# Cached attention on one core: the permutation of P moves from the normalization to the exponential's write and to the transposes' read

## The chip, the cores and the metric

The kernel runs on one core of a Trainium2 chip. The metric is the device time of one execution in microseconds (us); every time below is of that kind or comes from one profiled execution. Five engines work side by side, each through its own queue in order: TensorE (PE, with its weight loads shown apart as PEld), VectorE (DVE), ScalarE (ACT), GpSimd (POOL) and the queue SP, which here only issues transfers. They are held together by semaphores.

## The reference

There are two blocks, A and B, of the same form, and their outputs are put side by side. For each block, with 16 batches, 64 query rows, model width 640, 32 heads of 128 and 512 cached keys:

```python
q = (x @ wq).reshape(B, Sq, H, Dh).transpose(0, 2, 1, 3)
scores = einsum("bhqd,bhkd->bhqk", q, k_cache) * (Dh ** -0.5)
p = softmax(scores, axis=-1)
o = einsum("bhqk,bhkd->bhqd", p, v_cache)
out = o.transpose(0, 2, 1, 3).reshape(B, Sq, H * Dh) @ wo
```

All inputs and the output are bf16.

## The kernel before

Two batches are taken together, so that 2 x 64 query rows fill 128 partitions. One step g is one head of such a pair; two steps make a macro step m. There are 256 macro steps: 2 blocks x 2 halves of 16 heads x 8 pairs of batches x 8 macro steps. Every 8 macro steps a new group (a new pair of batches, or a new half or block) begins.

The order of each engine's work is written out by hand. A template per engine (class Cfg, lines 30 to 33) lists what the engine does in one slot and, beside each entry, how many macro steps ahead of the slot it works:

```python
PE_T = (("TR2", 1), ("QP2", 4), ("KX", 4, 0), ("SM2", 3), ("PV2", 1), ("XT", 0), ("OP2", 0), ("KX", 4, 1))
ACT_T = (("QE2", 4), ("OE2", 1), ("XE", 0), ("EX", 3, 0), ("EX", 3, 1), ("OV", 0), ("ST", -1))
DVE_T = (("TE2", 1), ("RC2", 2), ("KE", 4, 0), ("MX", 3, 0), ("MX", 3, 1), ("KE", 4, 1), ("OVF", 0))
POOL_T = (("NM", 0, 0), ("NM", 0, 1))
```

In the order of the data, for one macro step:

- KX (line 433) transposes the cached keys on TensorE, 8 tiles for each of the two batches; KE (line 442) copies them out of PSUM on VectorE.
- QP2 (line 451) projects the queries, QE2 (line 459) copies them out on ScalarE with the scale.
- SM2 (line 467) makes the scores of the two steps into two PSUM banks, one for each step (s_bank, line 424). There are only these two banks, so SM2 of the next macro step can begin only when both exponentials of this one have read them.
- MX (line 476, VectorE) takes the negated row maximum, one instruction for each step.
- EX (line 482, ScalarE) takes the exponential with that maximum as bias, writes P to p_ring in bf16 and sums the rows into rowsum; on the chip it is two instructions, an ACTIVATE and a short read of the accumulator.
- RC2 (line 488, VectorE) takes the reciprocals of both sums.
- NM (line 496, GpSimd) multiplies P with the reciprocal into pn_ring, one instruction for each step.
- TR2 (line 505) transposes 128 columns of pn_ring at a time, 4 tiles for each step, into PSUM; the tile of pn_ring is the stationary operand of these matrix products, which a weight load brings in, and the identity is streamed. TE2 (line 512, VectorE) copies the result out.
- PV2 (line 524) multiplies with the cached values, OE2 (line 532, ScalarE) copies out, OP2 (lines 540 and 545) projects into the output banks.
- XT (line 604) and XE (line 612) transpose the rows of x and copy them out on ScalarE, once for each group, so in 32 of the 256 slots.

The order of keys matters here. The keys come in so that column t x 64 + pp of the scores is key 8 pp + t (t below 8, pp below 64). The values come in so that partition p of tile t' holds key 4 p + t'. So the columns of P have to be put in another order on their way from the scores to the transposes. In this kernel NM does that: it reads P as it lies, (th, tl, pp), and writes pn_ring in the order (tl, pp, th), which is a step of 4 bytes between elements that are written one after the other. EX writes without a step, and TR2 loads 128 columns that lie side by side.

Of the kernel before, what the change touches and what calls it, by code (L numbers as in the profile page):

```python
# [7 lines left out]
ACTF = mybir.ActivationFunctionType  # L8
ALU = mybir.AluOpType
# [5 lines left out]
class Cfg:  # L15
# [9 lines left out]
    NP = 4  # L25
    NPN = 3
# [320 lines left out]
def mha_kernel(nc, blocks, out, cfg=None):  # L347
# [8 lines left out]
    scale = float(DH) ** -0.5  # L356
# [9 lines left out]
    NKB, NVB, NX, NXN, NQ, NKT, NP, NPN, NT, NO, NR = (cfg.NKB, cfg.NVB, cfg.NX, cfg.NXN, cfg.NQ, cfg.NKT, cfg.NP,  # L366
                                                       cfg.NPN, cfg.NT, cfg.NO, cfg.NR)
# [10 lines left out]
    with contextlib.ExitStack() as es:  # L378
        block = es.enter_context(nc.Block())

        def sb(name, shape, dt):
            return es.enter_context(nc.sbuf_tensor(name, shape, dt))
# [10 lines left out]
        p_ring = sb("p_ring", [128, NP, SK], BF16)  # L393
        pn_ring = sb("pn_ring", [128, NPN, SK], BF16)
# [3 lines left out]
        negmax = sb("negmax", [128, NR], F32)  # L398
        rowsum = sb("rowsum", [128, NR], F32)
        recip = sb("recip", [128, NR], F32)  # L400
        ones_sb = sb("ones_sb", [128, 128], BF16)
        ident = sb("ident", [128, 128], BF16)
# [15 lines left out]
        pt_ps = pt_ps_flat.rearrange("p (s t q) -> p s t q", s=2, t=4)  # L418
# [5 lines left out]
        def s_bank(sub):  # L424
            return ps[:, S_BANK0 + sub, :]
# [53 lines left out]
        def em_EX(e, op):  # L479
            g = op.idx  # L480
            r = g % NR
            ins = e.activation(p_ring[:, g % NP, :], s_bank(g % 2), ACTF.Exp, bias=negmax[:, r:r + 1], scale=1.0,  # L482
                               accum_out=rowsum[:, r:r + 1])
            return ins, ins

# [5 lines left out]
        def em_NM(e, op):  # L491
            g = op.idx
            r = g % NR
            src = p_ring[:, g % NP, :].rearrange("q (th tl pp) -> q th tl pp", th=2, tl=4)
            dst = pn_ring[:, g % NPN, :].rearrange("q (tl pp th) -> q th tl pp", tl=4, th=2)
            ins = e.tensor_scalar(dst, src, recip[:, r:r + 1], 1.0, ALU.mult, ALU.mult)  # L496
            return ins, ins

        def em_TR2(e, op):
            m = op.idx  # L500
            first = last = None
            for sub in range(2):
                g = 2 * m + sub
                for t in range(4):
                    ins = e.transpose(pt_ps[:, sub, t, :], pn_ring[:, g % NPN, t * 128:(t + 1) * 128], ident[:, :])  # L505
                    first = first or ins
                    last = ins
            return first, last
# [107 lines left out]
        def em_LDKV(e, op):  # L616
# [6 lines left out]
            else:  # L623
# [3 lines left out]
            return ins, ins  # L627

        emitters = dict(KX=em_KX, KE=em_KE, QP2=em_QP2, QE2=em_QE2, SM2=em_SM2, MX=em_MX, EX=em_EX, RC2=em_RC2,
                        NM=em_NM, TR2=em_TR2, TE2=em_TE2, PV2=em_PV2, OE2=em_OE2, OP2=em_OP2, OV=em_OV,  # L630
                        OVP=em_OVP, OVF=em_OVF, ST=em_ST, XT=em_XT, XE=em_XE, INIT1=em_INIT1, INIT2=em_INIT2,
                        LDWQ=em_LDWQ, LDWO=em_LDWO, LDX=em_LDX, LDK=em_LDKV, LDV=em_LDKV)
# [87 lines left out]
```

## Time and profile before

| | |
|---|---|
| time, median of 2 runs | 958.55 us (958.49 and 958.61) |
| span of the profiled execution | 956.8 us |
| mean granted TensorE clock | 0.998 of full speed |
| ScalarE busy | 567.1 us (59%) |
| GpSimd busy | 416.9 us (44%) |
| VectorE busy | 841.9 us (88%) |
| HBM | 311 GB/s over the span |
| copy of the values' transposes, line 512, mean | 682 ns |
| copy of queries, 128x256, line 459, mean | 384 ns |
| copy of x, 128x640 to bf16, line 612, mean | 702 ns |
| copy of partial outputs, 128x640 to f32, line 555, mean | 710 ns |
| read of the accumulator after EX, mean | 205 ns |
| weight load of any 128x128 tile, mean | 98 to 99 ns |

The span is the time from the first to the last instruction in one profiled execution; the timed runs are other executions, 1.7 to 1.8 us above it. A weight load overlaps the matrix products and the next loads, so its mean duration is not what one costs: the distance from one load to the next is. [...]

### The profile page before, as it was taken

The page shows a single profiled execution, that of the slowest core. Times are in us where ns is not written, and L with a number is a line of the kernel's source. Part 1 is how long each engine was busy: PE and PEld are TensorE (multiplying, and loading weights), DVE is VectorE, ACT ScalarE, POOL GpSimd, SP SyncE. Part 2 cuts the span into 40 slices and gives each one's busy share as a digit, 9 for nine tenths or more (in the row PEclk, how much of TensorE's full clock was granted, in tenths as well). Part 3 has the DMA queues.
Part 4 walks back from the last instruction along what each step waited for, and adds up shares of the span by engine and source line. Part 5 has one row for each costly group of instructions (what it writes and reads, how often), then busy time and mean ns, then how long its engine had stood idle before and what let it go on. Part 6 is the DMA issues. An engine that isn't in the chain of part 4 may idle for free.

```text
span 956.8 us, 34351 instructions
## 1 busy us (share of the span) xinstructions
PE 919.4 (96%) x14755; PEld 733.5 (77%) x15008; DVE 841.9 (88%) x1552; ACT 567.1 (59%) x1585; POOL 416.9 (44%) x518
## 2 busy tenths in 40 slices
PE   4999999999999999999999999999999999999997
PEld 3877777778777777877777787777877778777775
DVE  2898899898899999899999899889899998999996
ACT  1666656666665565656566666666666656565654
POOL 0444444444444444444444444444444444444443
PEclk9999999999999999999999999999999999999999
DMA  9999999999999999888999999988888988899830
GB/s 315 364 365 364 351 365 367 365 368 351 338 337 337 343 330 315 299 292 305 322 332 352 326 353 327 306 294 296 302 305 288 308 301 297 295 297 314 295 124 15
DMA packets 230871, 299.51 MB, mean 313 GB/s; under 512 B 9536, under 2 KB 165184, under 8 KB 230720
## 3 DMA queue, kind: packets, MB, share of 16 engines
q1 hardware_dynamic: 228416, 294.69, 91.0%
q8 instruction: 118, 1.93, 0.8%
q10 hardware_dynamic: 2304, 2.62, 0.8%
q14 instruction: 33, 0.27, 0.1%
HBM read 294.65 MB, written 2.62 MB: 311 GB/s over the span
## 4 chain that ended last, share of the span: by engine, by line
PE 89%; DVE 4%; POOL 3%; issue 2%; SPq 1%; DMA 1%; POOLq 0%; DVEq 0%
PE ps L433 22%; PE ps L524 14%; PE ps L451 14%; PE ps L467 14%; PE ps L505 12%; PE ps L545 7%; PE ps L540 5%; POOL pn_ring L496 3%; DVE out_sb L560 1%; DVE ktp_ring L442 1%; DVE pT_ring L512 1%; PE ps L604 1%; DMA xn_ring<-in_A_x_dram 1%; SPq L626 1%; SPq L583 1%
## 5 line engine op out<-in xcount | busy, mean ns | idle before, releaser
L496 POOL TENSOR_SCALAR pn_ring<-p_ring,recip 128x512 bf16<-128x512 bf16 x512 | 416.3, 843 | 532.7 <-DVE recip L488 532.7
L442 DVE COPY ktp_ring<-ps 128x1024 bf16<-128x1024 bf16 x512 | 353.7, 691 | 105.3 <-PE ps L433 85.1
L482 ACT ACTIVATE p_ring<-ps,negmax 128x512 bf16<-128x512 f32 x512 | 345.6, 684 | 4.8 <-DVE negmax L476 4.8
L476 DVE TENSOR_REDUCE negmax<-ps 128x1 f32<-128x512 f32 x512 | 327.3, 681 | 0.4 <-PE ps L467 0.3
L433 PE MATMUL ps<-ident,kn_ring 128*128 128x128 bf16 x4096 | 314.6, 220 | 2.8 <-DMA kn_ring<-in_A_k_cache_dram 1.6
L532 ACT ACTIVATE oT_ring<-ps 128x256 bf16<-128x256 f32 x256 | 98.0, 383 | 306.0 <-PE ps L524 306.0
L433 PEld LDWEIGHTS ps<-ident,kn_ring 128*128 128x128 bf16 x4096 | 251.9, 98 | 34.2 <-DVE ktp_ring L442 2.6
L524 PEld LDWEIGHTS ps<-pT_ring,v_ring 128*128 128x128 bf16 x4096 | 133.5, 98 | 109.2 <-issue 100.0
L451 PE MATMUL ps<-xT_ring,wq_sb 128*128 128x128 bf16 x2560 | 186.4, 220 | 3.2 <-DMA wq_sb<-in_A_wq_dram 3.2
L512 DVE COPY pT_ring<-ps 128x1024 bf16<-128x1024 bf16 x256 | 174.5, 682 | 4.6 <-PE ps L505 3.8
L524 PE MATMUL ps<-pT_ring,v_ring 128*128 128x64 bf16 x4096 | 163.8, 194 | 3.3 <-issue 1.7
L467 PE MATMUL ps<-ktp_ring,qT_ring 128*64 128x512 bf16 x1024 | 159.8, 392 | 0.4 <-ACT p_ring L482 0.4
L505 PE MATMUL ps<-ident,pn_ring 128*128 128x128 bf16 x2048 | 156.7, 219 | 3.5 <-POOL pn_ring L496 3.5
L451 PEld LDWEIGHTS ps<-xT_ring,wq_sb 128*128 128x128 bf16 x2560 | 155.2, 98 | 3.5 <-DMA wq_sb<-in_A_wq_dram 3.5
L459 ACT ACTIVATE qT_ring<-ps 128x256 bf16<-128x256 f32 x256 | 98.4, 384 | 66.8 <-PE ps L451 66.8
L505 PEld LDWEIGHTS ps<-ident,pn_ring 128*128 128x128 bf16 x2048 | 124.1, 98 | 7.0 <-POOL pn_ring L496 6.7
L545 PE MATMUL ps<-wo_sb,oT_ring 128*128 128x128 bf16 x512 | 112.1, 219 | 13.4
L482 ACT ACTIVATION_READ_ACCUMULATOR p_ring<-ps,negmax 128x1 f32 x512 | 105.0, 205 | 0.0
L540 PE MATMUL ps<-wo_sb,oT_ring 128*128 128x512 bf16 x259 | 97.8, 379 | 0.0
L540 PEld LDWEIGHTS ps<-wo_sb,oT_ring 128*128 128x128 bf16 x512 | 50.1, 98 | 30.6 <-ACT oT_ring L532 0.3
L467 PEld LDWEIGHTS ps<-ktp_ring,qT_ring 128*64 128x64 bf16 x1024 | 36.1, 108 | 27.1 <-ACT p_ring L482 0.6
L545 PEld LDWEIGHTS ps<-wo_sb,oT_ring 128*128 128x128 bf16 x512 | 50.1, 98 | 0.0
(13 smaller groups left out, 112.7 us busy)
## 6 DMA issues: line engine op xcount, KB each, us to landing
kn_ring<-in_A_k_cache_dram SPq DMA_DIRECT2D x128, 512.0 KB, 7.0
v_ring<-in_A_v_cache_dram SPq DMA_DIRECT2D x128, 512.0 KB, 7.2
kn_ring<-in_B_k_cache_dram SPq DMA_DIRECT2D x126, 512.0 KB, 4.8
v_ring<-in_B_v_cache_dram SPq DMA_DIRECT2D x126, 512.0 KB, 5.7
wq_sb<-in_A_wq_dram SPq DMA_DIRECT2D x8, 640.0 KB, 10.4
wo_sb<-in_A_wo_dram SPq DMA_DIRECT2D x8, 640.0 KB, 10.2
wq_sb<-in_B_wq_dram SPq DMA_DIRECT2D x8, 640.0 KB, 8.4
wo_sb<-in_B_wo_dram SPq DMA_DIRECT2D x8, 640.0 KB, 7.5
```

What stands on the lines that cost most here:

```text
L433: ins = e.transpose(kt_ps[:, t8, :], kn_ring[:, c % NKB, j, hp, t8, :], ident[:, :])
L442: ins = e.tensor_copy(dst, src)
L451: ins = e.matmul(q_ps[:, sub * 128:(sub + 1) * 128], wq_sb[:, ps_ % 2, kt, hh * DH:(hh + 1) * DH], xT_ring[:, grp % NX, kt, :], start=(kt ...
L467: ins = e.matmul(s_bank(sub)[64 * j:64 * j + 64, :], qT_ring[:, m % NQ, sub, 64 * j:64 * j + 64], ktp_ring[:, m % NKT, sub, j, :], start=T ...
L476: ins = e.reduce_max(negmax[:, r:r + 1], s_bank(g % 2), axis=AX.X, negate=True)
L482: ins = e.activation(p_ring[:, g % NP, :], s_bank(g % 2), ACTF.Exp, bias=negmax[:, r:r + 1], scale=1.0, accum_out=rowsum[:, r:r + 1])
L496: ins = e.tensor_scalar(dst, src, recip[:, r:r + 1], 1.0, ALU.mult, ALU.mult)
L505: ins = e.transpose(pt_ps[:, sub, t, :], pn_ring[:, g % NPN, t * 128:(t + 1) * 128], ident[:, :])
L512: ins = e.tensor_copy(pT_ring[:, m % NT].rearrange("p s t q -> p (s t q)"), pt_ps_flat)
L524: ins = e.matmul(o_ps[:, col:col + 64], v_ring[:, c % NVB, j, gi, t, :], pT_ring[:, m % NT, sub, t, 64 * j:64 * j + 64], start=(t == 0), s ...
L540: ins = e.matmul(out_ps0, oT_ring[:, m % NO, sub, :], wo_sb[:, ps_ % 2, hh, 0:N0], start=(hh == 0), stop=(hh == SPB - 1))
L545: last = e.matmul(out_ps1, oT_ring[:, m % NO, sub, :], wo_sb[:, ps_ % 2, hh, N0:DN], start=(hh == 0), stop=(hh == SPB - 1))
```

## The change

EX writes P in natural key order. Its source is the score bank as before, read from end to end; its destination is p_ring seen as (t, pp) with a step of 8 elements, 16 bytes, between elements that are written one after the other, in 8 runs of 64. NM loses both rearrangements and becomes one contiguous row in and out. TR2 takes every fourth column of pn_ring, a step of 8 bytes, in place of 128 columns side by side. The numbers of instructions, the queues' orders, the semaphores and the buffers stay.

```diff
         def em_EX(e, op):
             g = op.idx
             r = g % NR
-            ins = e.activation(p_ring[:, g % NP, :], s_bank(g % 2), ACTF.Exp, bias=negmax[:, r:r + 1], scale=1.0,
+            dst = p_ring[:, g % NP, :].rearrange("q (pp t) -> q t pp", t=8)
+            src = s_bank(g % 2).rearrange("q (t pp) -> q t pp", t=8)
+            ins = e.activation(dst, src, ACTF.Exp, bias=negmax[:, r:r + 1], scale=1.0,
                                accum_out=rowsum[:, r:r + 1])
...
         def em_NM(e, op):
             g = op.idx
             r = g % NR
-            src = p_ring[:, g % NP, :].rearrange("q (th tl pp) -> q th tl pp", th=2, tl=4)
-            dst = pn_ring[:, g % NPN, :].rearrange("q (tl pp th) -> q th tl pp", tl=4, th=2)
-            ins = e.tensor_scalar(dst, src, recip[:, r:r + 1], 1.0, ALU.mult, ALU.mult)
+            ins = e.tensor_scalar(pn_ring[:, g % NPN, :], p_ring[:, g % NP, :], recip[:, r:r + 1], 1.0, ALU.mult, ALU.mult)
...
                 g = 2 * m + sub
+                pn = pn_ring[:, g % NPN, :].rearrange("q (i t) -> q t i", t=4)
                 for t in range(4):
-                    ins = e.transpose(pt_ps[:, sub, t, :], pn_ring[:, g % NPN, t * 128:(t + 1) * 128], ident[:, :])
+                    ins = e.transpose(pt_ps[:, sub, t, :], pn[:, t, :], ident[:, :])
```

## The prediction, made before the changed kernel was run

> **What bounds the kernel now.** I read the page's busy table first, then the chain of waits, then the groups by line, and last the timeline of two neighbouring slots in the steady middle and of the last slots.
>
> ```profile
> PE 919.4 (96%) x14755; PEld 733.5 (77%) x15008; DVE 841.9 (88%) x1552; ACT 567.1 (59%) x1585; POOL 416.9 (44%) x518
> ...
> PE 89%; DVE 4%; POOL 3%; issue 2%; SPq 1%; DMA 1%; POOLq 0%; DVEq 0%
> ```
>
> TensorE is busy 96% of the span and carries 89% of the chain that ended last. GpSimd, on which the change takes a rearrangement away, is busy 44% and carries 3% of it.
>
> ```profile
> L496 POOL TENSOR_SCALAR pn_ring<-p_ring,recip 128x512 bf16<-128x512 bf16 x512 | 416.3, 843 | 532.7 <-DVE recip L488 532.7
> L442 DVE COPY ktp_ring<-ps 128x1024 bf16<-128x1024 bf16 x512 | 353.7, 691 | 105.3 <-PE ps L433 85.1
> L482 ACT ACTIVATE p_ring<-ps,negmax 128x512 bf16<-128x512 f32 x512 | 345.6, 684 | 4.8 <-DVE negmax L476 4.8
> L476 DVE TENSOR_REDUCE negmax<-ps 128x1 f32<-128x512 f32 x512 | 327.3, 681 | 0.4 <-PE ps L467 0.3
> ```
>
> NM (line 496) waits 532.7 us for its inputs, and the list of waits puts only 3.5 us of TensorE's idle time on it. EX (line 482) is 684 ns now. The timeline of one slot shows what lies around it (columns: start, duration in us, what ran, and in brackets the idle time before):
>
> ```profile
> 599.88 0.62 PE L467 MATMUL ps<-ktp_ring,qT_ring 128*64 128x512 bf16 x4
> ...
> 600.43 0.52 PEld L524 LDWEIGHTS ps<-pT_ring,v_ring 128*128 128x128 bf16 x16 [0.41 <-issue]
> 600.43 0.64 PE L524 MATMUL ps<-pT_ring,v_ring 128*128 128x64 bf16 x16
> 600.60 1.28 DVE L476 TENSOR_REDUCE negmax<-ps 128x1 f32<-128x512 f32 x2
> ...
> 601.39 0.68 ACT L482 ACTIVATE p_ring<-ps,negmax 128x512 bf16<-128x512 f32 x1
> ...
> 601.85 0.49 PEld L505 LDWEIGHTS ps<-ident,pn_ring 128*128 128x128 bf16 x8
> ...
> 602.62 0.21 ACT L482 ACTIVATION_READ_ACCUMULATOR p_ring<-ps,negmax 128x1 f32 x1
> ...
> 603.45 0.62 PE L467 MATMUL ps<-ktp_ring,qT_ring 128*64 128x512 bf16 x4
> ```
>
> A slot of TensorE is 603.45 - 599.88 = 3.57 us, without a gap. Inside it runs a loop that is not late yet. SM2 fills the score banks; MX reads them; EX0 begins 1.51 us after SM2 did (OE2 holds ScalarE just before); the second read of the accumulator ends at 602.83, 2.95 us after SM2's start; and the next SM2 may only then overwrite the banks. How long that last hand-over takes shows where SM2 does wait, among the last slots:
>
> ```profile
> 944.55 0.21 ACT L482 ACTIVATION_READ_ACCUMULATOR p_ring<-ps,negmax 128x1 f32 x1
> ...
> 944.83 0.17 PEld L467 LDWEIGHTS ps<-ktp_ring,qT_ring 128*64 128x64 bf16 x4 [0.57 <-ACT p_ring L482]
> ```
>
> The read ends at 944.76 and the first product of SM2 starts at 944.87 in the same view: 0.11 us. So the loop SM2 to SM2 takes 2.95 + 0.11 = 3.06 us, against 3.57: a slack of 0.51 us in a plain slot. In one slot of eight, XE lies ahead of EX on ScalarE: there SM2 starts at 603.45, the second read ends at 607.00 and the next SM2 starts at 607.29, so the slack is 0.29 - 0.11 = 0.18 us.
>
> **The change part by part.**
>
> **EX writes with a 16-byte step.** 512 ACTIVATEs, all inside this loop, two to a turn. Call the growth of one d. Each slot grows by 2d less its slack, or by nothing. With 224 plain slots and 32 with XE:
>
> added time = 224 x max(0, 2d - 0.51) + 32 x max(0, 2d - 0.18).
>
> TensorE works in order, so behind a late SM2 stand PV2, OP2, KX, TR2 and QP2, and nothing fills the gap. VectorE and GpSimd have their own turns through EX: from reciprocal to reciprocal (0.15 RC2 + 0.61 KE + 0.64 MX + 0.03 + 1.44 both EX + 0.03 = 2.90 us + 2d), and SM2 to TR2 (2.95 + 0.03 to RC2, 0.25 to NM, 1.62 both NM, 0.05 = 4.90 + 2d, against one slot plus the 1.97 us from the next SM2 to TR2, so 2.93 + 2d). Both are shorter than 3.06 + 2d and add nothing more.
>
> The trace has no ScalarE write with a step, so d is bounded. Below: zero. A partial-output copy of 640 elements to 4-byte f32 takes 710 ns, the copy of x to 2-byte bf16 702, so twice the bytes written cost ScalarE 8 ns. No reason for a gain: source, count and function stay. Above: from 384 ns at 256 elements and 702 at 640 comes 0.828 ns an element, 0.424 us for 512; a write that holds the engine for one more beat an element gives d = 0.424, for two more d = 0.848. The only row with a stepped write is NM's: 843 ns over 512 elements, 1.65 ns each, on another engine and with a step of 4 bytes; at that rate EX would gain 512 x (1.65 - 0.83) = 0.42 us. It is the nearest row and agrees with one beat more, so I take d = 0.424: 224 x 0.338 + 32 x 0.668 = 75.7 + 21.4 = 97 us. Two beats give 224 x 1.186 + 32 x 1.516 = 314 us.
>
> [...]
>
> **NM becomes contiguous.** 512 instructions of 843 ns. If the step is what makes it slower than ScalarE's 684, it falls to about that; if not, it stays. It saves nothing either way beyond the 3.5 us above, because what hides it is the 2.93 us loop against a slot of 3.57: NM could even grow by 0.64 us a pair before it counted. I take 0.
>
> **TR2's weight loads take every fourth column.** 2,048 loads. How fast loads can follow one another is seen in PV2: 16 in 0.52 us, the last one 0.098 long, so (0.52 - 0.098) / 15 = 0.028 us apart. TR2's eight take 0.49: 0.056 us apart, the pace of the streamed identity. So a load may take twice as long under that cover. Below: zero, as the matrix products set the pace. Above: 0.098 each if loads stop overlapping, 0.042 x 2,048 = 86 us; four times 0.028 is 0.112 and gives 0.056 x 2,048 = 115 us. I take 0, because even a load twice as slow, the price that NM's rate suggests for EX's write, stays hidden. It does not add to EX's cost: the slot would be 3.57 + 0.34 = 3.91 us against 3.06 + 0.85 = 3.91, and the longer of the two counts.
>
> **Sum**, against the profiled execution: 956.8 + 97.1 = 1053.9 us of span, and 1.75 us by which the median of the runs (958.55) stands above that span: 1056 us.
>
> **The rivals.**
>
> *The write's step is free.* d is zero or below 0.09 us, where even the XE slots have room; up to d = 0.13 the 32 slots cost 2.6 us. [...] Against it: the one stepped write in the trace runs at half ScalarE's rate. Then GpSimd's relief goes to its idle time: 955 to 961 us. This is the case on the other side, and it is decided at d = 0.25 us, where plain slots begin to stall.
>
> *The weight load becomes TensorE's bound,* with EX unchanged. For it: no load in the trace has a step, so nothing shows that 0.028 us holds. Against it: it needs more than twice that. 1045 to 1073 us.
>
> *The write is far worse,* d from 0.5 to 0.85: several writers and transfers at once (the DMA engines are 91% busy) may queue for one partition. 1095 to 1273 us.
>
> *A gain of over 2%* would need TensorE's slot itself to shrink; the trace has no gap in it that NM causes, beyond 3.5 us.
>
> **How the numbers follow.** A change of 2% is about what a measurement of this kernel can tell from no change. Forecast, d from 0.30 to 0.50 with 0.424 likeliest: 0.42, own range 993 to 1095 us. Free step: 0.33. Weight load alone: 0.10. Far worse: 0.12. Gain: 0.03. So slower 0.42 + 0.10 + 0.12 = 0.64, same 0.33, faster 0.03. The range goes from 954 us (3.5 us of waits for NM gone, and a little) to 1120 us, which is d = 0.55; left out are most of "far worse" and the gain, some 0.13.
>
> **What would show it.** Right: EX near 1.1 us in the groups (684 now), SM2 (line 467) with idle time ended by ScalarE of some 80 to 100 us in all (1.0 now), a slot of 3.9 us, and NM's waits longer. If EX stays under 0.93 us (d below 0.25) and the time moves little, the free step holds. If TR2's loads come more than 0.06 us apart and line 505 grows on the chain, the weight load is it. I am wrong in the loop if EX grows by 0.4 us and the slots do not, or if the stall sits at RC2 or TR2 while SM2 is on time.

## The result and the profile after

The changed kernel takes 1772.69 us (median of 2 runs, 1772.39 and 1772.99) against 958.55 us: a ratio of 1.850, with a 95% interval of 1.844 to 1.855. The forecast was 1056 us with a range of 954 to 1120 us. The direction was right; the time lies far outside the range, and the change is some eight times the forecast one (814 us for 97).

The page of the changed kernel, its busy table, its row of granted clock and its chain (lines below L482 have moved by two, below L496 by one):

```profile
PE 1106.2 (62%) x14755; PEld 850.3 (48%) x15008; DVE 857.0 (48%) x1552; ACT 1393.5 (79%) x1585; POOL 348.5 (20%) x518
...
PEclk8979998788897889878888889888878898798988
...
ACT 73%; PE 23%; issue 2%; SPq 1%; DMA 0%; POOL 0%; DVE 0%; POOLq 0%; DVEq 0%
ACT p_ring L484 67%; PE ps L467 11%; PE ps L525 11%; ACT oT_ring L533 5%; ACT xT_ring L613 1%; PE ps L605 1%; DMA xn_ring<-in_A_x_dram 0%; SPq L627 0%; SPq L584 0%; SPq L623 0%; POOL pn_ring L496 0%; PE ps L541 0%; DVE out_sb L561 0%; POOLq L378 0%; PE ps L506 0%
```

The engines have changed places. ScalarE went from 567 to 1393 us of busy time and carries 73% of the chain, nearly all of it in one line, the exponential. TensorE is idle 38% of the span, and its granted clock, 9 tenths throughout before (0.998 on the mean), now swings between 7 and 9; its mean is 0.867. Next the groups by line (count, then busy us and mean ns of one, then idle time before and what ended it):

```profile
L484 ACT ACTIVATE p_ring<-ps,negmax 128x512 bf16<-128x512 f32 x512 | 1234.8, 2657 | 2.2 <-DVE negmax L476 2.2
L496 POOL TENSOR_SCALAR pn_ring<-p_ring,recip 128x512 bf16<-128x512 bf16 x512 | 347.8, 692 | 1414.2 <-DVE recip L490 1414.2
L467 PE MATMUL ps<-ktp_ring,qT_ring 128*64 128x512 bf16 x1024 | 206.3, 492 | 617.5 <-ACT p_ring L484 617.5
```

EX takes 2657 ns where it took 684. NM fell from 843 to 692 ns. SM2's products wait 617.5 us for EX, and they are longer themselves, 492 ns. Before, they waited 0.4 us and took 392 ns:

```profile
L467 PE MATMUL ps<-ktp_ring,qT_ring 128*64 128x512 bf16 x1024 | 159.8, 392 | 0.4 <-ACT p_ring L482 0.4
```

The timeline of one slot in which TensorE has its full clock:

```profile
902.52 0.62 PE L467 MATMUL ps<-ktp_ring,qT_ring 128*64 128x512 bf16 x4 [2.79 <-ACT p_ring L484]
...
904.04 2.57 ACT L484 ACTIVATE p_ring<-ps,negmax 128x512 bf16<-128x512 f32 x1
...
906.10 0.50 ACT L484 ACTIVATION_READ_ACCUMULATOR p_ring<-ps,negmax 128x1 f32 x1
906.12 2.75 ACT L484 ACTIVATE p_ring<-ps,negmax 128x512 bf16<-128x512 f32 x1
908.37 0.50 ACT L484 ACTIVATION_READ_ACCUMULATOR p_ring<-ps,negmax 128x1 f32 x1
...
908.92 0.62 PE L467 MATMUL ps<-ktp_ring,qT_ring 128*64 128x512 bf16 x4 [2.76 <-ACT p_ring L484]
```

In the slot of the kernel before that the prediction shows, the second exponential is this line:

```profile
602.05 0.69 ACT L482 ACTIVATE p_ring<-ps,negmax 128x512 bf16<-128x512 f32 x1
```

The loop of the prediction can be read off term by term. EX0 begins 904.04 - 902.52 = 1.52 us after SM2 (1.51 before). The second exponential begins 2.08 us later (0.66 before), and the read of its accumulator ends 2.75 us after its own start (0.78 before). The next SM2 comes 0.05 us after that, where 0.11 was taken. Sum: 6.40 us a slot, for 3.57. The second exponential is printed as starting 0.49 us before the first one ends, so the printed durations of two neighbours overlap and do not add up to what the pair takes. Not all slots are like this one; the table by stretches shows two slots, with TensorE's busy time first and its granted clock as the third entry from the end:

```profile
417.50:423.90 6.40, 3.58 (x57) 2.81 (x58) 3.26 (x7) 5.91 (x8) 1.36 (x2) 1.00 0.75 239
...
430.30:437.53 7.23, 4.77 (x58) 3.46 (x59) 3.33 (x7) 5.32 (x7) 1.36 (x2) 0.80 0.56 185
```

The first has a clock of 1.00 and lasts 6.40 us; the second, at 0.80 on the mean, lasts 7.23 us. Of the 224 plain slots, 89 are of the second kind, told by an SM2 of 1.06 us in place of 0.62. The 0.80 is a mean. In the same table by stretches of 1 us the clock of the second slot is half at first and full later:

```profile
430.00:431.00 1.00, 0.70 (x4) 0.19 (x4) 0.72 (x2) 0.46 (x3) 0.46 (x1) 0.50 0.57 221
...
435.00:436.00 1.00, 0.29 (x6) 0.12 (x3) 0.16 (x1) 1.00 (x3) 0.00 (x0) 1.00 1.09 372
```

In this trace's record of the granted clock there are two values only, 1.0 and 0.5; it stands at 0.5 in 107 stretches of 3.41 or 6.83 us each (the last one, cut short by the end, 2.0), 473 us in all.

### The profile page after: what moved, and what is told of

Its sections match the earlier page's. It is cut to its first block, busy times and chain, and to the rows that moved or that the text cites. A ratio compares the mean times of both kernels' runs of the same rounds, so it can differ in the third digit from the quotient of the medians.

```text
span 1771.2 us, 34351 instructions
## 1 busy us (share of the span) xinstructions
PE 1106.2 (62%) x14755; PEld 850.3 (48%) x15008; DVE 857.0 (48%) x1552; ACT 1393.5 (79%) x1585; POOL 348.5 (20%) x518
## 4 chain that ended last, share of the span: by engine, by line
ACT 73%; PE 23%; issue 2%; SPq 1%; DMA 0%; POOL 0%; DVE 0%; POOLq 0%; DVEq 0%
ACT p_ring L484 67%; PE ps L467 11%; PE ps L525 11%; ACT oT_ring L533 5%; ACT xT_ring L613 1%; PE ps L605 1%; DMA xn_ring<-in_A_x_dram 0%; SPq L627 0%; SPq L584 0%; SPq L623 0%; POOL pn_ring L496 0%; PE ps L541 0%; DVE out_sb L561 0%; POOLq L378 0%; PE ps L506 0%
## 5 line engine op out<-in xcount | busy, mean ns | idle before, releaser
L484 ACT ACTIVATE p_ring<-ps,negmax 128x512 bf16<-128x512 f32 x512 | 1234.8, 2657 | 2.2 <-DVE negmax L476 2.2
L496 POOL TENSOR_SCALAR pn_ring<-p_ring,recip 128x512 bf16<-128x512 bf16 x512 | 347.8, 692 | 1414.2 <-DVE recip L490 1414.2
L467 PE MATMUL ps<-ktp_ring,qT_ring 128*64 128x512 bf16 x1024 | 206.3, 492 | 617.5 <-ACT p_ring L484 617.5
L490 DVE RECIPROCAL recip<-rowsum 128x2 f32<-128x2 f32 x256 | 42.4, 166 | 662.7 <-ACT p_ring L484 662.7
L433 PEld LDWEIGHTS ps<-ident,kn_ring 128*128 128x128 bf16 x4096 | 278.0, 105 | 48.3 <-issue 24.6
L484 ACT ACTIVATION_READ_ACCUMULATOR p_ring<-ps,negmax 128x1 f32 x512 | 261.6, 511 | 0.0
L525 PEld LDWEIGHTS ps<-pT_ring,v_ring 128*128 128x128 bf16 x4096 | 170.9, 111 | 148.0 <-issue 148.0
L525 PE MATMUL ps<-pT_ring,v_ring 128*128 128x64 bf16 x4096 | 205.4, 214 | 1.7 <-issue 1.7
L459 ACT ACTIVATE qT_ring<-ps 128x256 bf16<-128x256 f32 x256 | 173.9, 679 | 8.5 <-PE ps L451 8.5
L541 PEld LDWEIGHTS ps<-wo_sb,oT_ring 128*128 128x128 bf16 x512 | 59.6, 116 | 47.2 <-issue 29.2
```

The lines of the kernel that those rows point to most:

```text
L433: ins = e.transpose(kt_ps[:, t8, :], kn_ring[:, c % NKB, j, hp, t8, :], ident[:, :])
L467: ins = e.matmul(s_bank(sub)[64 * j:64 * j + 64, :], qT_ring[:, m % NQ, sub, 64 * j:64 * j + 64], ktp_ring[:, m % NKT, sub, j, :], start=T ...
L484: ins = e.activation(dst, src, ACTF.Exp, bias=negmax[:, r:r + 1], scale=1.0, accum_out=rowsum[:, r:r + 1])
L496: ins = e.tensor_scalar(pn_ring[:, g % NPN, :], p_ring[:, g % NP, :], recip[:, r:r + 1], 1.0, ALU.mult, ALU.mult)
L525: ins = e.matmul(o_ps[:, col:col + 64], v_ring[:, c % NVB, j, gi, t, :], pT_ring[:, m % NT, sub, t, 64 * j:64 * j + 64], start=(t == 0), s ...
L541: ins = e.matmul(out_ps0, oT_ring[:, m % NO, sub, :], wo_sb[:, ps_ % 2, hh, 0:N0], start=(hh == 0), stop=(hh == SPB - 1))
```

## The experiments

**Which part of the change it is.** First the exponential's step alone, in the kernel before.

```diff
-            ins = e.activation(p_ring[:, g % NP, :], s_bank(g % 2), ACTF.Exp, ...
+            dst = p_ring[:, g % NP, :].rearrange("q (pp t) -> q t pp", t=8)
+            src = s_bank(g % 2).rearrange("q (t pp) -> q t pp", t=8)
+            ins = e.activation(dst, src, ACTF.Exp, ...
```

> The kernel before with the exponential's 16-byte step alone; normalization and transposes stay as before, so the columns of P reach the transposes in another order than the values' keys. Theory: the exponential's write carries the whole loss, through the loop SM2 - maxima - exponentials - SM2. Then EX stays near 2.66 us, a slot near 6.4 us, and the time is 1750 to 1800 us, as with the whole change. Rival (the transposes' stepped weight loads or the contiguous normalization carry part of it): clearly below 1700 us.

Measured: 1776.04 us (one run). Its groups by line:

```profile
L484 ACT ACTIVATE p_ring<-ps,negmax 128x512 bf16<-128x512 f32 x512 | 1231.3, 2651 | 2.0 <-DVE negmax L476 2.0
L498 POOL TENSOR_SCALAR pn_ring<-p_ring,recip 128x512 bf16<-128x512 bf16 x512 | 417.6, 844 | 1347.0 <-DVE recip L490 1347.0
```

EX is as long as in the full change, NM is back at 844 ns, and the time is the same within 0.2%. The loss sits in EX's write. Then the rest alone:

```diff
-            ins = e.tensor_scalar(dst, src, recip[:, r:r + 1], 1.0, ALU.mult, ALU.mult)
+            ins = e.tensor_scalar(pn_ring[:, g % NPN, :], p_ring[:, g % NP, :], recip[:, r:r + 1], 1.0, ...
...
-                    ins = e.transpose(pt_ps[:, sub, t, :], pn_ring[:, g % NPN, t * 128:(t + 1) * 128], ident[:, :])
+                    ins = e.transpose(pt_ps[:, sub, t, :], pn[:, t, :], ident[:, :])
```

> The rest of the change alone: contiguous normalization and transposes of every fourth column; the exponential writes without a step, so P goes in with its keys in another order. Theory: TensorE's slot stays 3.57 us, NM takes near 0.69 us in place of 0.84, and the time is 953 to 959 us. Rival (stepped weight loads set TensorE's pace): loads of TR2 more than 0.056 us apart, 1040 us or more.

Measured: 954.59 us against 958.86, a ratio of 0.9955 (0.9938 to 0.9971). Groups by line, and one line of the timeline (start, duration):

```profile
L494 POOL TENSOR_SCALAR pn_ring<-p_ring,recip 128x512 bf16<-128x512 bf16 x512 | 347.9, 692 | 598.1 <-DVE recip L488 598.1
...
L504 PEld LDWEIGHTS ps<-ident,pn_ring 128*128 128x128 bf16 x2048 | 128.2, 114 | 2.4 <-POOL pn_ring L494 1.3 <-ACT xT_ring L611 0.2
```

```profile
601.10 0.50 PEld L504 LDWEIGHTS ps<-ident,pn_ring 128*128 128x128 bf16 x8
```

A load of every fourth column is printed at 114 ns for 98, but eight of them come in 0.50 us, (0.50 - 0.114) / 7 = 0.055 us apart, the pace of the streamed identity. Stepped weight loads cost nothing here. The rest of the change brings 4 us (2.8 to 5.9 by the interval), and most of it can be seen at NM. TR2's wait for NM, before and here (us in all, times, longest):

```profile
PE ps L505 <- POOL pn_ring L496: 3.5, 17, 0.6
```

```profile
PE ps L504 <- POOL pn_ring L494: 0.6, 2, 0.3
```

The longest plain slots in the steady part, 15 of some 4.08 us before, are 3.83 us.

**What in the write is dear.** Both kernels are the one before with another step of EX alone; the code is the first diff with t=2 and t=4.

> The kernel before with EX writing at a step of 2 elements, 4 bytes, in 2 runs of 256; the order of P's columns is another one. If the price goes by how many elements fall into one 16-byte stretch (here 4): EX within 0.1 us of 0.68 and the time near 959 us. If every 2-byte element that has no neighbour written with it costs the same: EX near 2.66 us and 1750 to 1800 us. If it goes with the step: EX near 0.684 + 1.97 x 4/16 = 1.18 us, and by the loop about 1100 us.

> The same at a step of 4 elements, 8 bytes, in 4 runs of 128; the order of P's columns is another one. If the price goes by the elements in one 16-byte stretch and two are enough: EX near 0.68 us, time near 959 us. If each lone element costs: EX near 2.66 us, 1750 to 1800 us. If it goes with the step: EX near 1.67 us and about 1350 us.

Measured: 959.01 and 1114.27 us (one run each, 958.86 before). EX with a step of 4 bytes, then of 8:

```profile
L484 ACT ACTIVATE p_ring<-ps,negmax 128x512 bf16<-128x512 f32 x512 | 410.0, 835 | 4.8 <-DVE negmax L476 4.8
```

```profile
L484 ACT ACTIVATE p_ring<-ps,negmax 128x512 bf16<-128x512 f32 x512 | 664.0, 1407 | 2.2 <-DVE negmax L476 2.2
```

With 684, 835, 1407 and 2651 ns at 2, 4, 8 and 16 bytes none of the three expectations holds. From 8 to 16 bytes EX grows by 1244 ns, which fits 0.163 us + 4.86 ns for every visit to a 16-byte stretch (a visit: the writing comes to another 16 bytes; 256 visits at 8 bytes, 512 at 16), but just as well a price on the distance itself. The step of 4 bytes also shows that the slack in the loop is real: EX grew by 0.15 us and the time stayed. Next a larger step (t=16), and 8 runs without a step:

```diff
+            dst = p_ring[:, g % NP, :].rearrange("q (b a pp) -> q a b pp", a=2, b=4)
+            src = s_bank(g % 2).rearrange("q (a b pp) -> q a b pp", a=2, b=4)
```

> The kernel before with EX writing at a step of 16 elements, 32 bytes, in 16 runs of 32; the order of P's columns is another one. Steps of 4, 8 and 16 bytes gave 0.835, 1.407 and 2.651 us. Theory line: what costs is each 16-byte stretch that an instruction touches, about 4.86 ns, however many elements of it are written in passing (0.163 + 512 x 4.86 ns / elements per stretch gives 0.785, 1.41, 2.65). Then 32 bytes cost what 16 do: EX near 2.65 us and the time near 1775 us. Theory step: the price grows with the distance itself (0.1555 us per byte of step): EX near 5.14 us and the time near 2700 us.

> The kernel before with EX writing 8 runs of 64 elements without a step inside a run, the runs in another order; the order of P's columns is another one. Both theories of the step: EX within 0.05 us of 0.684 and the time near 959 us. Rival (the number of runs, or a pattern of several dimensions, costs): EX clearly longer, with 8 runs as in the change near 2.65 us.

Measured: 1681.87 and 958.47 us (one run each, 958.55 before). EX at 32 bytes, then in runs:

```profile
L484 ACT ACTIVATE p_ring<-ps,negmax 128x512 bf16<-128x512 f32 x512 | 1174.1, 2527 | 2.2 <-DVE negmax L476 2.2
```

```profile
L484 ACT ACTIVATE p_ring<-ps,negmax 128x512 bf16<-128x512 f32 x512 | 345.6, 684 | 4.8 <-DVE negmax L476 4.8
```

Twice the distance costs no more, a little less even (2527 ns; why is open): the price goes with the visits and not with the distance. Runs of 64 in another order are free (684 ns, as in a row). Next, whether the visit itself is dear or the half word in it, and whether the round number of 16 matters. In the first kernel p_ring holds f32 and EX writes with t=4; in the second, the changed kernel, a row of 8 elements gets a ninth that stays empty, so the step is 18 bytes.

```diff
-        p_ring = sb("p_ring", [128, NP, SK], BF16)
+        p_ring = sb("p_ring", [128, NP, SK // 8, 9], BF16)
...
+            dst = p_ring[:, g % NP, :, 0:8].rearrange("q pp t -> q t pp")
```

> P kept in 4-byte f32, EX writing at a step of 4 elements, 16 bytes, in 4 runs of 128; normalization and transposes as before, so the order of P's columns is another one; one buffer fewer for the values (4 for 5), to make room. Theory line: one element in each 16-byte stretch, EX near 2.65 us, time near 1775 us. Rival (what costs is a 2-byte element that fills only half a 4-byte word): EX near 0.69 us, time 955 to 985 us, with the rest of the doubt from the missing buffer.

> The changed kernel with rows of 9 elements for 8 in p_ring, so EX writes at a step of 18 bytes and NM reads the 8; one buffer fewer for the values (4 for 5), to make room. Theory line: still one element in each 16-byte stretch, EX near 2.65 us and the time 1750 to 1800 us. Rival (steps that are multiples of 16 bytes, or powers of two, come back to the same bank of the memory): EX well below, 0.7 to 1.4 us, time 955 to 1120 us. Theory step: EX near 2.96 us, time near 1890 us.

Measured: 1021.13 and 1772.39 us (one run each). EX in f32 at 16 bytes, then in bf16 at 18:

```profile
L484 ACT ACTIVATE p_ring<-ps,negmax 128x512 f32<-128x512 f32 x512 | 565.2, 1186 | 4.3 <-DVE negmax L476 2.2
```

```profile
L484 ACT ACTIVATE p_ring<-ps,negmax 128x512 bf16<-128x512 f32 x512 | 1226.5, 2638 | 2.2 <-DVE negmax L476 2.2
```

A step of 18 bytes changes next to nothing (2638 ns for 2651), which speaks against the rival of the round step. But the f32 write, with just as many visits, takes 1186 ns and neither of its two expected values: with the fixed part of the bf16 fit, a visit costs (1.186 - 0.163) / 512 = 2.0 ns with a whole 4-byte word in it and 4.86 ns with a 2-byte half. That predicts that pairs of bf16 are cheap:

```diff
+            dst = p_ring[:, g % NP, :].rearrange("q (pp t u) -> q t pp u", t=4, u=2)
+            src = s_bank(g % 2).rearrange("q (t pp u) -> q t pp u", t=4, u=2)
```

> The kernel before with EX writing pairs of neighbouring elements (one 4-byte word) at a step of 16 bytes between pairs, 256 pairs, in 4 runs of 64; the order of P's columns is another one. Theory: a 16-byte stretch costs 4.86 ns when a 2-byte half of a word is written in it and about 2.0 ns when whole words are (from f32 at 16 bytes, (1.186 - 0.163) us / 512). Then 256 x 2.0 = 0.51 us hardly shows over ScalarE's own 0.42: EX 0.68 to 0.80 us, time near 959 us. Rival (a stretch costs 4.86 ns whatever is written): EX near 0.163 + 256 x 4.86 ns = 1.41 us, time near 1114 us, as with the 8-byte step.

Measured: 959.86 us (one run, 958.95 before). EX:

```profile
L484 ACT ACTIVATE p_ring<-ps,negmax 128x512 bf16<-128x512 f32 x512 | 361.1, 723 | 4.6 <-DVE negmax L476 4.6
```

The write still jumps 16 bytes between 256 visits, the number that cost 1407 ns with half words at a step of 8 bytes. In pairs it costs 723 ns. So the price depends on two things: visits to 16-byte stretches, and whether an element fills its 4-byte word.

**The same order without the dear write.** The changed kernel with the step moved to the read in PSUM, and with pairs:

```diff
+            dst = p_ring[:, g % NP, :].rearrange("q (pp t) -> q pp t", t=8)
+            src = s_bank(g % 2).rearrange("q (t pp) -> q pp t", t=8)
```

> The changed kernel with the step on the other side: EX writes P in natural key order without a step and reads the score bank in PSUM at a step of 64 f32 (256 bytes), in runs of 8. Theory: only the write in SBUF is dear; the read costs at most what the f32 write at a 16-byte step did (EX 1.19 us, 1021 us). If it is free: EX near 0.684 and the time 953 to 957 us, under both kernels. Rival (any step of ScalarE costs the same on either side): EX near 2.65 us, time near 1770 us.

```diff
+            dst = p_ring[:, g % NP, :].rearrange("q (pp t u) -> q t pp u", t=4, u=2)
+            src = s_bank(g % 2).rearrange("q (t u pp) -> q t pp u", t=4, u=2)
```

> The changed kernel with EX writing natural key order in pairs: it reads the score bank in pairs 64 f32 apart and writes two neighbouring elements, 16 bytes from pair to pair. Theory as for the pairs above, if the read's step is free: EX 0.68 to 0.80 us, time 953 to 960 us. If a step in the PSUM read costs by itself, EX is longer here than in the run with pairs and no step in the read, by up to half of what it costs in the run with the stepped read alone.

Measured: with the stepped read 954.75 us against 958.95, a ratio of 0.9956 (0.9939 to 0.9972); in pairs 953.94 us (one run). The stepped read's groups and its wait of TR2 for NM (us in all, times, longest), and the pairs' EX:

```profile
L496 POOL TENSOR_SCALAR pn_ring<-p_ring,recip 128x512 bf16<-128x512 bf16 x512 | 349.3, 695 | 595.4 <-DVE recip L490 595.4
L484 ACT ACTIVATE p_ring<-ps,negmax 128x512 bf16<-128x512 f32 x512 | 346.3, 686 | 4.8 <-DVE negmax L476 4.8
```

```profile
PE ps L506 <- POOL pn_ring L496: 0.6, 2, 0.3
```

```profile
L484 ACT ACTIVATE p_ring<-ps,negmax 128x512 bf16<-128x512 f32 x512 | 363.7, 734 | 4.8 <-DVE negmax L476 4.8
```

A read of f32 in PSUM at a step of 256 bytes costs EX 2 ns, 686 for 684. This version does what the change does, keys in natural order, contiguous NM, strided transposes, and is 4 us faster than the kernel before, as much as the rest of the change alone brought, and 818 us faster than the changed kernel.

**The clock.** TensorE is given more work in the changed kernel where it waits:

```diff
-            for t8 in range(8):
+            for t8 in list(range(8)) * (6 if j == 0 else 1):
```

> The changed kernel with the first key transposes of each macro step done six times over (the same 8 products, 2.2 us more of TensorE's work where it waits 2.8 us a slot). Theory: 89 of the 224 plain slots are 7.2 us and not 6.4 because TensorE, idle for nearly half of each slot, gets a lower clock (mean 0.867), which stretches SM2 and PV2 inside the loop. With the filler the clock is 0.98 or more, plain slots are 6.4 us, and the time is 1680 to 1710 us, although TensorE does more. Rival (the long slots have another cause, or the clock lies off the loop): 1765 us or more.

Measured: 1695.62 us (one run), 77 us less than the changed kernel although TensorE does 10,240 products more. Groups by line:

```profile
L484 ACT ACTIVATE p_ring<-ps,negmax 128x512 bf16<-128x512 f32 x512 | 1243.5, 2675 | 4.0 <-DVE negmax L476 4.0
...
L467 PE MATMUL ps<-ktp_ring,qT_ring 128*64 128x512 bf16 x1024 | 159.6, 392 | 156.0 <-ACT p_ring L484 156.0
```

EX is as slow as in the changed kernel, SM2 is back at 392 ns, the mean granted clock is 0.997, and the 224 plain slots average 6.43 us (6.73 in the changed kernel, 3.60 before). Whether the length of a gap or TensorE's idle share lowers the clock is not separated: the filler takes away both. At the 8-byte step, with 254 waits of SM2 of 0.57 us on the mean, the clock was 0.995.

## Why the prediction was wrong

- **What bounds the kernel, and the loop: right.** SM2, maxima, exponentials, SM2 was named as the loop that would become late, with 3.06 us + 2d against 3.57. With the growth that the timeline shows, 1.42 us from start to start and 1.97 for the second, it gives 3.06 + 3.39 = 6.45 us; measured 6.40. The printed growth of the row, 1.97 us for each of the two, would have given 7.00, because the two overlap. It also fits the smaller cases: with the starts and ends of EX at the 8-byte step, 0.52 + 0.63 of growth gives 4.21 us, measured 4.17.
- **The term that failed: d.** "I take d = 0.424" was the price of EX's stepped write; the row shows 1.97 us, the loop 1.42 and 1.97. The bound "for two more d = 0.848", meant as the far end, was too low as well, and no run shows the growth of 0.30 to 0.50 us for a bf16 write at 16 bytes, the case that was given the largest chance. No row before the change shows its lower end of 0.30 us (993 us) either: it was the author's estimate, and the runs showed 1.97 us in its place. Behind it stood a misread row. NM's 1.65 ns an element was taken for the price of a stepped write, but NM without a step is still 692 ns: only 151 of its 843 ns were the step. That step was 4 bytes, four elements to a 16-byte stretch; EX at that same step also grew by 151 ns. The row was right for a step of 4 bytes and said nothing of one of 16.
- **The evidence against a cost was no evidence.** That f32 output took only 8 ns more than bf16 showed that more bytes in a row cost next to nothing. In a row every word is whole, so it could not show the dear case.
- **A term was missing: the clock.** With the measured growth the prediction's formula gives 224 x (3.39 - 0.51) + 32 x (3.39 - 0.18) = 748 us, and 956.8 + 748 + 1.75 = 1706 us, within 1% of the 1695.62 us with TensorE kept busy. The other 77 us come from TensorE's idle time, 2.8 us in a slot at full clock: the clock is then halved for 3.41 or 6.83 us, which stretches SM2 (1.06 us for 0.62) and PV2, and they are inside the loop. The filler shows that it is the idle time.
- **NM: right.** Nothing beyond 3.5 us was expected of it; 4 us came from the rest of the change together, 2.9 of them where TR2's waits for NM went.
- **Weight loads: right.** They stayed under the streamed identity, 0.055 us apart, so the rival of the weight load falls.
- **The rival "far worse" came nearest, but neither its size nor its reason holds.** Its upper end of 1273 us was too low, and several writers queuing for a partition is not what the runs show: EX stays within 2536 and 2778 ns from the first instruction to the last, when hardly anything else runs.
- **Stretches of 16 bytes.** The 16 bytes fit the runs: from a step of 8 bytes to one of 16 EX goes from 1407 to 2651 ns, and beyond 16 it grows no more, with 2638 at 18 and 2527 at 32. Two elements to a stretch do not make the write free: at 8 bytes, with two, EX takes 1407 ns for 684. Less the fixed 0.163 us of the fit, ScalarE's f32 write costs 2.0 ns an element against 0.83 in a row (the prediction's rate from the copies), 2.4 times, and the bf16 write 4.86, 5.9 times.

What stays open is why a half word costs more than a whole one, and why the 32-byte step costs a little less than the one of 16. A stepped write from VectorE was not tried.

## What to carry to other kernels

A permutation belongs where it is free or nearly so: here in the read from PSUM (2 ns more), or in pairs that fill a 4-byte word (39 ns more, which the loop's slack hides), and not in a 2-byte write with a long step (2651 ns for 684 at 16 bytes). A price that is taken from the nearest row has to be taken as a difference, the same instruction with and without the feature, and at the same step; NM's whole rate hid that its step was a small part. And when the forecast makes TensorE wait a large part of every slot, here 2.8 us of 6.4, the clock is a term of the sum, here 77 us.

## What the runs showed of the hardware

- ScalarE writing bf16 to SBUF: 684 ns for 512 elements in a row, 835, 1407 and 2651 ns at steps of 4, 8 and 16 bytes, 2638 at 18, 2527 at 32. From 8 to 18 bytes 0.163 us + 4.86 ns for every visit to a 16-byte stretch fits within 1%; at 4 bytes it gives 0.785 us, 6% too little, and at 32 bytes 2.65 us, 5% too much. These are printed durations, which overlap: from the start of the first EX to the end of the second read a pair takes 1.44 us in a row, 2.60 at 8 bytes and 4.83 at 16 (the first and the last are medians, of the kernel before and of the changed one), so there a visit costs (4.83 - 2.60) / 512 = 4.4 ns. Whole 4-byte words cost less: 1186 ns for 512 f32 at 16 bytes, 723 ns for 256 bf16 pairs at 16 bytes.
- ScalarE reading f32 from PSUM at a step of 256 bytes: 686 ns, as without.
- Weight loads of every fourth bf16 column: printed 16 ns longer (114 for 98), no further apart (0.055 us for 0.056).
- TensorE's clock: with waits of some 2.8 us in every 6.4 it went down to half for 3.41 or 6.83 us at a time, so that two slots of five had 0.80 on the mean. With TensorE kept busy by the filler the mean clock was 0.997 and the time 77 us less; with 254 waits of 0.57 us on the mean, at the 8-byte step, the mean clock stayed at 0.995. The longest wait of all in the changed kernel, 3.7 us, came only at the end, near 1751 us.
